# A linear-attention block with a gated feed-forward branch: joint inner products in the last projection, a new chunk layout, and phi's relu on another engine

## The chip, the cores and the metric

The kernel runs on one core of one Trainium2 chip. The metric is the device time of one execution in microseconds (us); for each kernel the median of several executions is given. TensorE is called PE, its weight loads PEld, VectorE DVE, ScalarE ACT, GpSimd POOL, and SyncE, which issues all DMAs here, SP.

## The reference

x is 2048 tokens by 1024 features, in bf16. After a layer norm two branches are computed and joined:

```python
phi = lambda t: where(t > 0, t + 1, exp(t)) + 1e-6
q, k, v = xn @ wqkv            # 32 heads of 32
kv = phi(k).T @ v              # per head
o  = phi(q) @ kv / (phi(q) @ sum(phi(k)) + 1e-6)
s  = o @ wo
g  = silu((silu(xn @ w_gate) * (xn @ w_up)) @ w_down)    # hidden width 3584
out = x + s * g
```

## The kernel before

Nearly every matrix product is made by a seven-product scheme of Strassen's kind. A product of 2 x 2 blocks is made from seven block products of sums and differences of the blocks (R00, R10, R01, R11, T1 to T4 on the token side; A.. and S3, S5, S6, S7 on the weight side) instead of eight. Class `Pair` (line 718) carries it out for a pair of results w = 0, 1: `step(w, m)` makes product m in PSUM, and the results leave through `evac` after products 2, 7, 3 and 4. After products 2, 3 and 4 the evacuation reads PSUM (kind "ps"); product 7's result passes through an SBUF tile first (kind "sb"). Products named in the set J are made for both w at once, by a second level of the same scheme inside: seven *inner* products of 256 columns, whose operands are again sums and differences of quarters. `fresh` (line 748) does this for products 1 and 5 in four steps; `early` (line 857) lists those steps alternately for 5 and 1, and `late` the rest. In `fresh` two ACT copies and two DVE additions of 256 columns lie between the PE steps.

The work goes in stages: layer norm with keys and values (K stage), queries (Q stage), gate and up projections, the attention output s, and last the down projection. Intermediate h and s go to memory and come back.

*phi* is made by `phi_evac` (line 1031): ACT makes exp of the PSUM result into an SBUF tile (line 470), DVE takes min(., 1) + 1e-6 (line 1034), and DVE adds max(src, 0), reading the source again (line 1036). It is used for keys in `kv_out` (line 1047, called with c = 0 or 1 for the two halves of the keys) and for queries in `q_pair` (line 1262): 32 evacuations each.

*The down stage* (lines 1416 to 1584) goes through four couples of token tile pairs, each couple of two pairs w = 0, 1. For each pair it makes the token side's combinations T1 to T4 on DVE (`DProv.comb`, in halves of 896 elements) and then products 1, 5, 6, 2, 7, 3, 4, each 14 matmuls of 128 x 128 weights by 512 columns. Here the tokens are the stationary operand and the down weights move. Each couple needs four chunks of h of 896 KB (`h_load`), in six places `HC`; those of the next couple are loaded after product 5. In the first pair DVE also makes the weight sums S6, S7 and S3 (`wd_comb`). Each of the 32 results is evacuated by `d_pair`: ACT makes silu of the PSUM bank, DVE multiplies by s (loaded by DMA, 128 KB) and adds x (loaded 256 KB at a time), and a DMA stores it.

*What sets the order.* Each operation is first listed with its reads and writes. A planner (class `Plan`) then puts the operations of each engine and of SP in a fixed order by a model of their durations: the one that can start first, by deadline among those that are ready. PE may take operations from a window of 20. A DMA is placed some 12 us ahead of need unless it is marked `asap`. Operations of DVE whose operands are all in SBUF are marked `port`, and the model lets them and POOL's operations exclude each other. On the chip each engine then runs its list in that order, and semaphores hold it where something is not ready. Temporary tiles come from pools of slots: F2 (9 of 2 KB), F1 (4 of 1 KB), H1 (12 of 1 KB) and the 8 PSUM banks; a slot that has been free longest is taken first.

Of the kernel before, what the change touches and what calls it, by code (L numbers as in the profile page):

```python
# [13 lines left out]
KB = 1024  # L14
# [27 lines left out]
class VB:  # L42

    __slots__ = ("pool", "slot", "ops", "left", "armed", "leaves", "r", "id")
    count = 0

    def __init__(self, pool, armed=False, leaves=True):
        self.pool, self.armed, self.leaves = pool, armed, leaves
        self.slot = None
        self.ops = []  # L50
        VB.count += 1
        self.id = VB.count
        self.r = Region([("vb", self.id)])
# [6 lines left out]
class Plan:  # L60
# [62 lines left out]
    def schedule(self):  # L123
# [15 lines left out]
        for o in ops:  # L139
            o.npred = len(o.preds)  # L140
            o.ready = 0.0
            for v in o.vbs:
                if v.ops[0] is o:
                    v.left = len(v.ops)
                    v.pool.pend.append(o.idx)
# [12 lines left out]
        def place(o, t):  # L158
            got = []
            when = o.ready  # L160
            for v in o.vbs:
                if v.slot is not None:
                    continue
                P = v.pool
                mine = [k for u, k in got if u.pool is P]
                if len(P.free) <= bisect_left(P.pend, o.idx) + len(mine):
                    return inf, None
                c = None
                for k in P.free:
                    if v.armed and not P.armed[k] or k in mine:  # L170
                        continue
                    m = max(P.time[k], t)
                    key = (m, P.armed[k] and not v.armed, P.time[k], k)
                    if c is None or key < c[0]:
                        c = (key, k)
                if c is None:
                    return inf, None
                got.append((v, c[1]))
                when = max(when, P.time[c[1]])
            return when, got  # L180
# [118 lines left out]
def build_kernel(nc, A_x, A_wqkv, A_wo, B_w_gate, B_w_up, B_w_down, out, WINDOW=20, NWARM=12, NIDLE=5, LEAD=12.0):  # L299
# [8 lines left out]
    CS, IS = ("dve",) * 4, ("pool",) * 8  # L308
    UBANK, PU = 0.0, 6.0
    N0, NA, WA = 3, 2, True  # L310
    GC0 = ("dve",) * 4
# [10 lines left out]
    with ExitStack() as es:  # L322
# [82 lines left out]
        for k in range(F2.n):  # L405
            for hl in range(4):
                dsem("rr%d_%d" % (k, hl))
        for P in (F2, H1):
            for k in range(P.n):
                dsem("%s_%d" % (P.name, k))  # L410
# [65 lines left out]

        def tt(reads, writes, o, a, b, alu, n, fast=False, eng="dve"):
            f = lambda h: h.tensor_tensor(ev(o), ev(a), ev(b), alu)  # L478
            if eng == "pool":
                return op("pool", reads, writes, f, n / 531.0 + 0.2)  # L480
            q = dve(reads, writes, f, n, 1.92 if fast else 0.96)

            q.port = not any(isinstance(x, VB) and x.pool is BANK for x in reads)
            return q
# [545 lines left out]

        def phi_evac(reads, src, kind, out_ap, out_r):
            e = tmp(H1)
            act(reads, [e], partial(vap, e, FP16), src, ACT.Exp, 512, kind)
            dve([e], [e], lambda h: h.tensor_scalar(vap(e, FP16), vap(e, FP16), 1.0, EPS_PHI, ALU.min, ALU.add),  # L1034
                512, 3.84, urgent=PU).port = True
            dve(reads + [e], [out_r], lambda h: h.scalar_tensor_tensor(  # L1036
                out_ap, ev(src), 0.0, vap(e, FP16), ALU.max, ALU.add), 512, urgent=PU).port = kind == "sb"
# [9 lines left out]
        def kv_out(q, c, reads, src, kind):  # L1047

            if c < 2:
                o = pk_at[q % 4] + c * KB  # L1050
                phi_evac(reads, src, kind, SB.at(o, KB), SB.reg(o, KB))
            else:
# [209 lines left out]
        def q_pair(p, s, wf, at=(), mix=()):  # L1262
            def evac(w, i, j, src, v, kind):
                g = 2 * (2 * s + w) + i
                o, orr = pq_tile(p, g, j)
                phi_evac([v], src, kind, o, orr)
            ST.pair(Pair(Prov(wf, XV[p]), evac, JQ), at, mix)
# [147 lines left out]

        HC = [80, 112, R2, 96, 88, 104]
        HT = [120, 123.5, 127, 74]
        GB = 3584

        def hchunk(c):  # L1420
            o = HC[c] * KB
            return SB.at(o, 2 * GB, FP16).rearrange("p (n t) -> p n t", t=256), o

        def hpart(c, w, lo=0, hi=14):
            v, o = hchunk(c)
            keys = []
            for n in range(lo, hi):
                keys += SB.reg(o + n * 512 + w * 256, 256).keys
            return v[:, lo:hi, w * 128:(w + 1) * 128], Region(keys)

# [4 lines left out]
        def h_load(p, cc, f, c, **kw):  # L1435
            v, o = hchunk(c)
            dma([named("h", p, f)], [SB.reg(o, 2 * GB)], v,
                h_scr[p, f].rearrange("p (n t) -> p n t", t=512)[:, :, cc * 256:(cc + 1) * 256], dsem("hc%d" % c), 896 * KB, **kw)

        class DProv:  # L1440
# [5 lines left out]
            def form(self, nm, lo=0, hi=14):  # L1446
                if nm in ("T2", "T3"):
                    return htile(self.t[nm == "T3"], lo, hi)
                return hpart(self.ch[{"R00": 0, "R10": 1, "T4": 1, "R01": 2, "T1": 2, "R11": 3}[nm]], self.w, lo, hi)

# [5 lines left out]
            def full(self, w, m):  # L1456
                out_ = []
                for lo, hi in ((0, 4), (4, 7), (7, 10), (10, 14)):
                    v, r = self.form(XOF[m], lo, hi)
                    prs, rd = [], [r]  # L1460
                    for n in range(lo, hi):
                        wv, wr = wd_run(WDM[m], n, n + 1, BF16 if WDM[m][0] == "A" else FP16)
                        prs.append((v[:, n - lo, :], wv[:, 0, :]))
                        rd.append(wr)
                    out_.append((prs, rd))
                return out_

        def d_pair(p, m, prov):
            xo = {}

            def evac(w, i, j, src, v, kind):
                t = p * 8 + j * 4 + m
                g, s = tmp(H1), tmp(H1)
                dma([named("s", t, i)], [s], partial(vap, s, FP16), s_scr[t, i], vsem(s), 128 * KB)
                act([v], [g], partial(vap, g, FP16), src, ACT.Silu, 512, kind)
                tt([g, s], [g], partial(vap, g, FP16), partial(vap, g, FP16), partial(vap, s, FP16), ALU.mult, 512, True)
                if j not in xo:
                    q = xo[j] = tmp(F2)
                    dma([], [q], partial(vap, q), xf[t * 128:(t + 1) * 128, :], vsem(q), 256 * KB)
                q = xo[j]  # L1480
                xv = partial(vap, q, BF16, i * KB, KB)
                tt([g, q], [q], xv, partial(vap, g, FP16), xv, ALU.add, 512, True)
                dma([q], [], of[t * 128:(t + 1) * 128, i * 512:(i + 1) * 512], xv, vsem(q), 128 * KB, asap=True)
            return Pair(prov, evac)

# [60 lines left out]

        cur, spare = [0, 2, 1, 3], [4, 5]
        tw = [0]
        pend = []

        def chunks(p, cc, cur, late):
            for f in (0, 2, 1, 3):
                if (f in (1, 3)) == late or late is None:
                    h_load(p, cc, f, cur[f])
        chunks(0, 0, cur, None)
        for q, (p, cc) in enumerate(couples):
            last = None
            for w in range(2):
                t = [(0, 1), (2, 3)][tw[0] % 2]
                tw[0] += 1  # L1560
                pv = DProv(list(cur), w, t)
                pv.comb("T1", "R01", "R00")
                pv.comb("T2", "R11", "T1")
                pv.comb("T3", "T2", "R00")
                P = d_pair(p, 2 * cc + w, pv)
                nxt = couples[q + 1] if q < 3 else None
                for m in (1, 5, 6, 2, 7, 3, 4):
                    P.step(0, m)
                    if m == 2:
                        pv.comb("T4", "R10", "T2")  # L1570
                    if q == 0 and w == 0 and m == 1:
                        wd_comb("S6", "S5", "A00", ALU.subtract, FP16, BF16)
                        wd_comb("S7", "A11", "S6", ALU.subtract, BF16, FP16)
                        wd_comb("S3", "A10", "S6", ALU.subtract, BF16, FP16)
                    if nxt and w == 0 and m == 5:
                        ncur = [spare[0], cur[0], spare[1], cur[2]]
                        h_load(nxt[0], nxt[1], 0, ncur[0])
                        h_load(nxt[0], nxt[1], 2, ncur[2])
                    if nxt and w == 1 and m == 5:
                        h_load(nxt[0], nxt[1], 1, ncur[1])  # L1580
                        h_load(nxt[0], nxt[1], 3, ncur[3])
            if nxt:
                spare = [cur[1], cur[3]]
                cur = ncur

# [67 lines left out]
```

## Time and profile before

| | |
|---|---|
| median of 3 executions | 748.47 us (747.05 to 748.60) |
| the profiled execution | 745.33 us |
| its span, first to last instruction | 743.6 us |
| PE busy | 712.8 us (96%), 4092 matmuls |
| DVE busy | 567.2 us (76%) |
| ACT busy | 357.9 us (48%) |
| POOL busy | 262.0 us (35%) |

The profile is of one execution, with its own time. Busy time is given per engine; matmuls overlap their neighbours, so that a busy PE isn't necessarily at its peak, and the distance from start to start says more than the duration of one (379 ns at 512 columns, 273 at 256). A group's line has line, engine, operation, output<-input, shape and count, then busy us, mean ns of one, and the engine's idle time just before it with what ended it. In a windows view, each row is a stretch of time with its length and each engine's busy us and number of instructions in it. `ps` is a PSUM bank, `SB` the large SBUF array. Some matmul records, a few per cent, are missing from a trace.

### The profile page before, as it was taken

What the parts mean: (1) busy time and instruction counts of PE and PEld (TensorE: products, weight loads), DVE (VectorE), ACT (ScalarE), POOL (GpSimd) and SP (SyncE); (2) the same over time, 40 slices, a digit from 0 to 9 for tenths busy, and PEclk for the clock granted to TensorE, in tenths of its full rate; (3) what the DMA queues carried; (4) which work ended last, traced back from release to release, by engine and by line L of the source; (5) the groups of instructions that cost most, each with busy time, mean ns of one, the idle gap of its engine ahead of it and who ended that gap; (6) DMA issues with size and microseconds to landing.
All of it is one profiled execution on the core that took longest, in us unless ns stands there. A gap on an engine that the chain in (4) does not pass through costs nothing.

```text
span 743.6 us, 11430 instructions
## 1 busy us (share of the span) xinstructions
PE 712.8 (96%) x4092; PEld 385.8 (52%) x4121; DVE 567.2 (76%) x1107; ACT 357.9 (48%) x677; POOL 262.0 (35%) x230
## 2 busy tenths in 40 slices
PE   8999999788999899999999999999999999999996
PEld 4444544344465565566666566566554444444442
DVE  6999766999989899887888888889978562533523
ACT  3567644765646677755545455454664111111111
POOL 2021000137548655876658747520740000000000
PEclk9999999999999999999999999999999999999999
DMA  9844205130233465475331233344698372927421
GB/s 303 206 77 109 44 0 169 52 121 4 67 117 128 153 207 180 133 264 169 104 109 50 93 107 107 93 139 153 214 318 246 114 213 84 277 79 217 125 76 42
DMA packets 139672, 101.54 MB, mean 137 GB/s; under 512 B 18784, under 2 KB 132704, under 8 KB 139616
## 3 DMA queue, kind: packets, MB, share of 16 engines
q1 hardware_dynamic: 139616, 100.82, 45.2%
q8 instruction: 32, 0.52, 0.3%
q14 instruction: 24, 0.20, 0.1%
HBM read 68.16 MB, written 29.49 MB: 131 GB/s over the span
## 4 chain that ended last, share of the span: by engine, by line
PE 75%; DVE 17%; DMA 3%; issue 2%; ACT 2%; SPq 0%; ACTq 0%; DVEq 0%
PE ps L420 75%; DVE SB L478 8%; DVE SB L1036 3%; DVE ps L478 2%; DVE SB L1034 2%; ACT SB L470 1%; DMA SB<-in_A_x_dram 1%; DMA SB<-q_scratch 1%; DMA SB<-SB 1%; DVE stats L995 1%; DVE stats L994 1%; SPq L490 0%; DVE Zh L1205 0%; ACT ps L470 0%; DVE SB L1201 0%
## 5 line engine op out<-in xcount | busy, mean ns | idle before, releaser
L420 PE MATMUL ps<-SB 128*128 128x512 f16 (+3 forms) x3971 | 702.4, 337 | 21.6 <-ACT ps L470 7.7
L420 PEld LDWEIGHTS ps<-SB 128*128 128x128 f16 (+1 forms) x4000 | 379.9, 98 | 342.6 <-DVE SB L478 15.0
L478 POOL TENSOR_TENSOR SB<-SB 128x1024 f16<-128x1024 bf16 (+3 forms) x196 | 247.9, 1292 | 226.5 <-PE ps L420 113.8
L470 ACT ACTIVATE SB<-ps 128x256 f32<-128x256 f32 (+4 forms) x397 | 213.0, 558 | 170.1 <-PE ps L420 157.1
L478 DVE TENSOR_TENSOR SB<-SB 128x512 f16<-128x512 f16 (+10 forms) x312 | 197.7, 662 | 71.7 <-DMA out_dram<-SB 20.6
L478 DVE TENSOR_TENSOR SB<-ps,SB 128x256 f32<-128x256 f32 (+2 forms) x318 | 181.4, 590 | 51.7 <-PE ps L420 41.0
L478 DVE TENSOR_TENSOR ps<-ps,SB 128x512 f32<-128x512 f32 (+1 forms) x238 | 122.2, 529 | 30.7 <-PE ps L420 23.4
L470 ACT ACTIVATE ps<-ps 128x512 f32<-128x512 f32 (+1 forms) x166 | 81.8, 494 | 124.7 <-PE ps L420 95.4
L470 ACT ACTIVATE SB<-SB 128x512 f16<-128x512 f32 (+1 forms) x68 | 42.2, 621 | 79.5 <-DVE SB L478 76.6
L998 POOL TENSOR_TENSOR rstd<-veps,neg_half 128x1 f32<-128x1 f32 x16 | 11.5, 721 | 63.6 <-DVE veps L997 61.0
L1034 DVE TENSOR_SCALAR SB<-SB 128x512 f16<-128x512 f16 x64 | 23.5, 383 | 11.9 <-ACT SB L470 11.9
L1036 DVE SCALAR_TENSOR_TENSOR SB<-ps,SB 128x512 bf16<-128x512 f32 x49 | 32.4, 678 | 0.1
L470 ACT ACTIVATE SB<-SB,zc 128x512 bf16<-128x512 bf16 x32 | 22.2, 715 | 3.2 <-DVE SB L478 3.0
L470 ACT ACTIVATE SB<-SB,nmr,rstd 128x1024 f16<-128x1024 bf16 x12 | 14.7, 1234 | 1.9 <-DVE nmr L1000 1.8
L994 DVE BATCH_NORM_STATS2 stats<-SB 128x6 f32<-128x512 bf16 x16 | 10.9, 683 | 3.4 <-DMA SB<-in_A_x_dram 3.4
L1036 DVE SCALAR_TENSOR_TENSOR SB<-SB 128x512 bf16<-128x512 f32 x15 | 12.5, 842 | 0.0
L995 DVE BATCH_NORM_STATS2 stats<-SB 128x6 f32<-128x512 bf16 x16 | 10.9, 680 | 0.0
L420 PE MATMUL ps<-SB,ident 128*128 128x512 f16 x17 | 6.4, 550 | 1.4 <-POOL ident L501 1.4
L449 PE MATMUL ps<-ident,SB 128*128 128x128 f16 x40 | 3.1, 220 | 1.7 <-DVE SB L1201 1.1
L420 PEld LDWEIGHTS ps<-SB,ident 128*128 128x128 f16 x17 | 2.1, 130 | 4.5 <-issue 2.8
L1286 DVE RECIPROCAL SB<-SB 128x64 f32<-128x64 f32 x8 | 4.3, 539 | 0.0
L449 PEld LDWEIGHTS ps<-ident,SB 128*128 128x128 f16 x40 | 2.4, 98 | 3.6 <-DVE SB L1004 1.6
(28 smaller groups left out, 24.8 us busy)
## 6 DMA issues: line engine op xcount, KB each, us to landing
h_scratch<-SB SPq DMA_DIRECT2D x112, 128.0 KB, 2.3
SB<-h_scratch SPq DMA_DIRECT2D x16, 896.0 KB, 6.5
SB<-in_A_x_dram SPq DMA_DIRECT2D x32, 256.0 KB, 3.2
SB<-in_B_w_gate_dram SPq DMA_DIRECT2D x14, 512.0 KB, 4.1
SB<-in_B_w_up_dram SPq DMA_DIRECT2D x14, 512.0 KB, 5.4
SB<-in_B_w_down_dram SPq DMA_DIRECT2D x4, 1792.0 KB, 8.7
SB<-in_A_wqkv_dram SPq DMA_DIRECT2D x12, 512.0 KB, 8.4
SB<-r_scratch SPq DMA_DIRECT2D x32, 128.0 KB, 2.8
```

What stands on the lines that cost most here:

```text
L420: last = h.matmul(o() if callable(o) else o, l() if callable(l) else l, r() if callable(r) else r, start=st, stop=sp, skip_group_check=True)
L449: last = h.transpose(o(), i(), ident[:, :])
L470: return op("act", reads, writes, lambda h: h.activation(ev(o), ev(i), func, **kw), n / 1200.0 + (0.055 if src == "ps" else 0.095) + (0.09 ...
L478: f = lambda h: h.tensor_tensor(ev(o), ev(a), ev(b), alu)
L994: dve([xr] + ([named("ve", 0)] if q == 1 else []), [sA], lambda h: h.bn_stats(stats[:, j, 0, :], xa[:, 0:512]), 512)
L995: dve([xr] + ([named("ve", 0)] if q == 1 else []), [sB], lambda h: h.bn_stats(stats[:, j, 1, :], xa[:, 512:1024]), 512)
L998: pool([ver, nh_r], [rsr], lambda h: h.tensor_tensor(rstd[:, j, :], veps[:, j, :], neg_half[:, :], ALU.pow), 0.56)
L1034: dve([e], [e], lambda h: h.tensor_scalar(vap(e, FP16), vap(e, FP16), 1.0, EPS_PHI, ALU.min, ALU.add), 512, 3.84, urgent=PU).port = True
L1036: dve(reads + [e], [out_r], lambda h: h.scalar_tensor_tensor(out_ap, ev(src), 0.0, vap(e, FP16), ALU.max, ALU.add), 512, urgent=PU).port = ...
L1286: dve([ea], [ra], lambda h, q=q: h.reciprocal(vap(ra, F32)[:, q * 64:q * 64 + 64], vap(ea, F32)[:, q * 64:q * 64 + 64]), 400)
```

## The change

Two things change. First, phi's relu: where `relu` is set, ACT makes it from the same source into a second tile, and DVE adds the two SBUF tiles. That is the case for the first half of the keys (c = 0) and for those query evacuations that read PSUM.

```diff
+    RQ = lambda w, i, j, kind: kind == "ps"
+    RK = lambda q, c, kind: c == 0
...
-        def phi_evac(reads, src, kind, out_ap, out_r):
+        def phi_evac(reads, src, kind, out_ap, out_r, relu=False):
             e = tmp(H1)
             act(reads, [e], partial(vap, e, FP16), src, ACT.Exp, 512, kind)
             dve([e], [e], lambda h: h.tensor_scalar(vap(e, FP16), vap(e, FP16), 1.0, EPS_PHI, ALU.min, ALU.add),
                 512, 3.84, urgent=PU).port = True
+            if relu:
+                r = tmp(H1)
+                act(reads, [r], partial(vap, r, FP16), src, ACT.Relu, 512, kind)
+                tt([e, r], [out_r], out_ap, partial(vap, e, FP16), partial(vap, r, FP16), ALU.add, 512, True)
+                return
             dve(reads + [e], [out_r], lambda h: h.scalar_tensor_tensor(
                 out_ap, ev(src), 0.0, vap(e, FP16), ALU.max, ALU.add), 512, urgent=PU).port = kind == "sb"
```

Second, the down stage. The first couple is made as before. In the other three, both pairs of a couple are one `Pair` with J = (1, 5): products 1 and 5 are made jointly by inner products. `DJProv.inner` makes the token side's inner sums for a couple (four additions of 896 elements for each of the two products), `wd_inner` the weight side's, once (eight of 1792 elements, one of each four in place). T1 to T4 are made for both pairs at once, with halves of 1792. After the joint steps come products 2, 6, 7, 3, 4, each for w = 0 and then w = 1.

Memory is laid out anew. There are five chunk places instead of six; a next couple's chunk goes into the only spare place (f = 0) or into one that this couple has finished with (f = 2 after T1, f = 3 after product 7, f = 1 after product 3), and is marked `asap`. T2 has a place of its own, T3 takes that of R00. The inner sums lie in gaps, and, from the second couple on, in two slots of F2 and four of H1 (`gone`), which are taken for good when the first such sum is made: a tile with `only=k` can have slot k alone, and a sum that holds several of them starts when all are free. An evacuation loads its 128 KB of x itself, into a slot of F1.

```diff
-        HC = [80, 112, R2, 96, 88, 104]
-        HT = [120, 123.5, 127, 74]
+        HC = [80, 112, 199, 96, 87]
+        HT = [119, 122.5, 103, 106.5]
+        H2 = 103
+        HI_AT = [73.5, 75.25, 77, 94, 110, 129.5, 194, 195.75]
+        WI_AT = [70, 160, 163.5, 126, 119, 122.5]
+        gone = [VB(F2, only=k) for k in range(2)] + [VB(H1, only=k) for k in range(8, 12)]
...
+        def wd_inner(m):
+            raw = BF16 if WDM[m][0] == "A" else FP16
+            R = {(h, u): wq(m, h, u, raw) for h in range(2) for u in range(2)}
+            d = wq(m, 0, 1, FP16)
+            t2, t3, t4 = (wi(m, f) for f in range(3))
+            for o, a, b in ((t3, R[1, 1], R[0, 1]), (d, R[0, 1], R[0, 0]), (t2, R[1, 1], d), (t4, R[1, 0], t2)):
+                tt([a[1], b[1]], [o[1]], o[0], a[0], b[0], ALU.subtract, 1792, True, hold=gone[:2] if m == 1 else ())
...
+            def inner(self, m):
+                B = {(k, w): self.form(XOF[m], 7 * k, 7 * k + 7, w) for k in range(2) for w in range(2)}
+                n0, n1, n2, s5 = (self.hi(m, f) for f in range(4))
+                for o, a, b, alu in ((n1, B[0, 0], B[0, 1], ALU.subtract), (s5, B[0, 1], B[1, 1], ALU.add),
+                                     (n0, s5, B[0, 0], ALU.subtract), (n2, B[1, 0], n0, ALU.subtract)):
+                    tt([a[1], b[1]], [o[1]], o[0], a[0], b[0], alu, 896, True, hold=gone[2:] if m == 5 else ())
...
-                g, s = tmp(H1), tmp(H1)
+                g, s, x = tmp(H1), tmp(H1), tmp(F1)
...
+            ncur = [spare, cur[3], cur[2], cur[0]]
+            if q == 0:
...
+                        if w == 0 and m == 5:
+                            load(1, 0, ncur[0])
+                        if w == 1 and m == 5:
+                            load(1, 2, ncur[2])
+                            load(1, 3, ncur[3])
+                            wd_inner(1)
+                            wd_inner(5)
+                        if w == 1 and m == 3:
+                            load(1, 1, ncur[1])
+            else:
+                pv = DJProv(list(cur))
+                P = d_pair(p * 8 + 2 * cc, pv, (1, 5))
+                pv.inner(1)
+                pv.comb("T1", "R01", "R00")
+                pv.inner(5)
+                load(q + 1, 0, ncur[0])
+                for _, st in P.early():
+                    st()
+                pv.comb("T2", "R11", "T1")
+                pv.comb("T3", "T2", "R00")
+                load(q + 1, 2, ncur[2])
+                for m in (2, 6, 7, 3, 4):
+                    for w in range(2):
+                        P.step(w, m)
+                    if m == 2:
+                        pv.comb("T4", "R10", "T2")
+                    if m == 7:
+                        load(q + 1, 3, ncur[3])
+                    if m == 3:
+                        load(q + 1, 1, ncur[1])
+            spare, cur = cur[1], ncur
```

## The prediction

> **What bounds the kernel now.** I read the down stage first, since most of the diff lies there. The chain that ended last, from 540 us on, starts with its shares by line (first fence, first line). Then it names only matmuls until the last three steps, which are the last evacuation. The windows view (second fence) has 92 to 94 matmuls of 512 columns in every 20 us and DVE mostly idle.
>
> ```profile
> by line: PE ps L420 96.5%; issue 0.4%; DVE SB L478 0.4%; ACT SB L470 0.3%
> ...
> 705.71 10.74 PE ps L420 x49
> 716.45 0.05 issue
> 716.50 10.74 PE ps L420 x49
> ```
>
> ```profile
> core 0: us, PE busy (x) PEld busy (x) DVE busy (x) ACT busy (x) POOL busy (x), PEclk, DMA share, GB/s
> 20.00:60.00 40.00, 37.50 (x193) 16.73 (x196) 38.24 (x92) 25.19 (x40) 5.02 (x6) 1.00 0.60 137
> 140.00:200.00 60.00, 52.19 (x339) 26.44 (x339) 58.41 (x117) 38.13 (x76) 30.64 (x23) 1.00 0.23 70
> ...
> 600.00:620.00 20.00, 19.89 (x92) 9.06 (x93) 9.47 (x20) 3.60 (x6) 0.00 (x0) 1.00 0.56 164
> ```
>
> So the down stage is bound by the number of PE columns alone. Start to start, neighbouring 512-column matmuls in the trace stand 215 or 216 ns apart; 784 of them (8 tile pairs x 7 products x 14) are 169.0 us, and counted back from PE's end at 737.6 the stage began at 568.7 and couple 1 begins at 568.7 + 2 x 21.1 = 610.9.
>
> Where phi is evacuated it is otherwise: in the K stage (20 to 60 us) and the Q stage (140 to 200 us) DVE is busy 96% and 97% and PE idles 2.5 and 7.8 us. The timeline of the Q stage shows two costs that the relu edit trades, and a collision:
>
> ```profile
> 169.78 4.62 POOL L478 TENSOR_TENSOR SB<-SB 128x512 f16<-128x512 f16 x4
> ...
> 170.54 4.02 DVE L1034 TENSOR_SCALAR SB<-SB 128x512 f16<-128x512 f16 x4
> ...
> 191.14 2.47 DVE L1036 SCALAR_TENSOR_TENSOR SB<-ps,SB 128x512 bf16<-128x512 f32 x4
> 193.54 1.08 DVE L478 TENSOR_TENSOR SB<-SB 128x512 f16<-128x512 f16 x3
> ```
>
> Four of the old last steps of phi take 2.47 us, a single one 0.68, so one follows the next after (2.47 - 0.68)/3 = 0.60. Of plain SBUF additions three take 1.08, one 0.42: 0.33 each. But at 170.5 four tensor_scalars of SBUF data, each 0.20 when undisturbed, take 4.02 us beside four POOL additions, and PE waits 2.2 us behind them. The groups by form give the average of it: the tensor_scalar from 120 to 200 us, and, over the whole kernel, a two-input operation of SBUF data against the same with one input in PSUM (number after the bar: busy us, mean ns).
>
> ```profile
> L1034 DVE TENSOR_SCALAR SB<-SB 128x512 f16<-128x512 f16 x32 | 14.5, 487 | 1.7 <-ACT SB L470 1.7
> ```
>
> ```profile
> L478 DVE TENSOR_TENSOR SB<-ps,SB 128x512 f16<-128x512 f32 x84 | 57.3, 683 | 9.2 <-ACT SB L470 8.6 <-PE ps L420 0.2
> ...
> L478 DVE TENSOR_TENSOR SB<-SB 128x512 f16<-128x512 f32 x28 | 30.7, 1097 | 0.0
> ```
>
> The form with an input in PSUM is not stretched; the one of SBUF alone is.
>
> [...] ten 256-column matmuls take 1.25 us at 345.28, one 0.272, so (1.25 - 0.272)/9 = 0.109. [...]
>
> **The change part by part.**
>
> *Joint products, PE.* A couple's products 1 and 5 were 2 x 2 x 14 = 56 matmuls of 512: 56 x 0.2155 = 12.07 us. They become 2 x 7 x 7 = 98 of 256: 98 x 0.109 = 10.68. Every one loads its weights; 98 ns of load fit under 109, and runs of twelve keep that pitch. Gain 1.39 us, three couples: **-4.2 us**, all of it on the path, since nothing else ends there. The first couple stays as it was.
>
> *Chain within the joint steps.* Elsewhere these steps are woven with the pair before; here 98 stand nearly alone, products 5 and 1 alternating. A step of two inner products takes PE 1.53 us; in that time ACT's 256-column copies (0.37 and 0.38) or DVE's addition (0.42) must come back[...]. Some 0.7 us is spare; a 1.1 us combination just ahead on DVE costs at most 0.4. Two or three such hits: +0.3 at most +1; I take **0**, as the model orders DVE around them, and keep +1.
>
> *Combinations on DVE.* Interpolating the 896-wide (620 ns) and 2048-wide (1213) rows, a 1792-wide one is 1.08 us. New once: 8 of these for the weights, 8.6 us. New per couple: 8 of 896, 5.0 us; T1 to T4 halve in number and double in width: equal. In couples 2 and 3 DVE has over 20 of 41 us free and the chunks land a whole phase ahead: 0. In the switch from couple 0 to 1 it is tight. The third chunk (f=2) now goes into the place of T1, free once the second tile's product 5 is done: 589.8 + 6.0 = 595.8. Landing takes 6.1 us in the median (8.3 at most), behind another 896 KB that may be ahead on SP's queue (up to 3.8 at the 241 GB/s of 590 to 612): 602 to 606. T1 (2.2) and the first two additions of inner(5) (1.2) follow, with some 2 us of evacuations between: 607 to 611.5, due 610.9. **+0.5 us**, from 0 to 2. Its cover is the weights being done by then: 16 us of new DVE work, of which 4 to 7 can go before 590, in 20 us with 6 to 8 us of other work. Behind a chunk load that waits on SP's queue stand s and x loads and output stores; PE waits for none of them.
>
> *Slots.* From here F2 loses two slots and H1 four. PE waits for none directly: silu frees the bank, and it needs one of 8 H1 slots where about 5 are in use. x comes in 32 loads of 128 KB instead of 16 of 256: SP issues 16 more of 0.43 us, 7 us in 170; behind them stand the s and h loads and the stores. F1 has 4 slots; load 3.2, add and wait about 1.5, store 1.9 with its queue about 2: under 9 us a round, so 4 slots give an evacuation every 2.2 us; the closest need is one in 3.0. 0.
>
> *phi's relu, K stage.* 16 evacuations. DVE gives up 0.60 and takes 0.33: -0.27 each. ACT gains one 512-column read of PSUM, 0.50 to 0.595: 8 us in a stage where it is 63% busy. About half fall before 55 us, where the chain runs through DVE: -2.0 at best; afterwards PE is full and nothing counts. POOL is nearly idle, so no collision. PE waits for ACT too there: I take **-0.8** (0 to -2.0).
>
> *phi's relu, Q stage.* 24 evacuations (products 2, 3, 4 of 32 in all). Undisturbed: 24 x -0.27 = -6.4 us of DVE. But the old step reads PSUM and keeps 0.60 beside POOL; the new addition is SBUF alone, and POOL is busy 51%. The tensor_scalars there average 487 ns, 0.2 us over the 0.28 of an undisturbed one. With 0.2 on each addition: 24 x (0.53 - 0.60) = -1.6 us. ACT rises from 38.1 to 50 of 60 us; behind the relus queue the copies and drains that PE waits for, 5 to 6 us in all of these 60. For it: the bank is free after two ACT reads instead of after three steps on two engines. I take **-1.2**; from below -5 (no collision), from above +9.6 (each addition meets a POOL operation as the four at 170.5 did: 1.0 us, 24 x 0.4).
>
> Sum: -4.2 + 0 + 0.5 - 0.8 - 1.2 = -5.7 us. The profiled execution took 745.33 (span 743.6, 1.7 around it) and would take 739.6. It lies 3.1 under the median of the runs, 748.47, which becomes **742.8**. About 0.2%, 1.5 us, is what a measurement can tell from none.
>
> **Rivals.**
> - *Relu brings nothing* (K and Q cancel against ACT's queue): -3.7, 744.8. For it: 51% POOL; against: the earlier bank.
> - *Relu brings its full worth*: Q -5, K -1.5, so -10.2, 738.3. For it: DVE at 97%; against: the collision seen at 170.5.
> - *The switch stalls.* inner(5) may start only when H1's slots 8 to 11 are free together; slots are handed out oldest first, and about four of twelve are in use by s loads made up to 12 us ahead. If the four are scattered it waits for a lull, up to some 5 us; PE can run product 1's steps meanwhile but without the alternation. +4.5: -1.2, 747.3, no change.
> - *Slower[...].* Q's additions at 1.0 on an engine that is 97% busy: +9.6 - 0.8 - 3.7 = +5.1, 753.6. It ends level at an addition of 0.60 + 4.5/24 = 0.79 us and is slower beyond 0.85. Against it: order is made by a plan that counts an SBUF addition and POOL as excluding each other, and DVE has other work to put in between.
>
> **How the numbers follow.** Forecast 0.52 (own range 740.5 to 744.5), nothing from relu 0.19, full worth 0.08, stalled switch 0.12, slower 0.09. Faster 0.79, within 0.2% 0.12, slower 0.09. Forecast and first rival hold 0.71; to 739.0 and 747.2, half of the two next on either side come in, 0.81.
>
> **What would show it.** Right: the down stage's PE in 164.8 us: 616 matmuls of 512 columns and 294 of 256; no PE gap above 1 us near 611; DVE's line 1036 with about 24 instructions instead of 64 in all; PE's idle time in 140 to 200 us down by 1 to 2. Wrong: new SBUF additions of phi averaging over 0.8 us; ACT over 90% in the Q stage; PE waiting for an addition of inner(5) or a chunk at the switch; 256-column pitch above 115 ns when they stand alone.

## The result, and the profile after

| | before | changed |
|---|---|---|
| median of 4 executions | 747.87 us | 748.22 us (746.96 to 749.63) |
| ratio, 95% interval | | 1.0005 (0.9981 to 1.003) |
| profiled execution, span | 745.33, 743.6 us | 749.63, 747.9 us |

No change that can be measured, where 5.7 us less was forecast (742.8 from 748.47). The profiled execution of the changed kernel is the slowest of its four and that of the kernel before a fast one, so stages are compared by their own lengths and the verdicts rest on medians and ratios.

The windows view of the changed kernel, for the stretches shown of before:

```profile
core 0: us, PE busy (x) PEld busy (x) DVE busy (x) ACT busy (x) POOL busy (x), PEclk, DMA share, GB/s
20.00:60.00 40.00, 40.00 (x221) 19.24 (x220) 38.65 (x99) 29.60 (x48) 5.57 (x8) 1.00 0.58 139
140.00:200.00 60.00, 50.81 (x307) 27.07 (x308) 53.15 (x115) 46.19 (x97) 30.99 (x24) 0.97 0.23 68
600.00:620.00 20.00, 20.00 (x119) 11.36 (x117) 15.18 (x25) 3.54 (x7) 0.00 (x0) 1.00 0.57 166
```

In the K stage PE no longer idles between 20 and 60 us. In the Q stage DVE fell from 58.4 to 53.2 us of 60 and ACT rose from 38.1 to 46.2, as the edit would have it. But PE is busy 50.8 us where it was 52.2, and its clock is no longer full (0.97). The groups from 120 to 200 us say what became of phi on DVE:

```profile
L1038 DVE TENSOR_SCALAR SB<-SB 128x512 f16<-128x512 f16 x32 | 15.4, 503 | 2.8 <-ACT SB L474 2.8
L482 DVE TENSOR_TENSOR SB<-SB 128x512 bf16<-128x512 f16 x23 | 8.7, 416 | 0.0
```

These 23 of the 24 new additions take 416 ns each, as undisturbed ones do (418 in e8 below, where POOL is busy 17.2 us from 125 to 200 us, 31.1 in e5). The last one falls just outside: it starts at 200.08 us beside POOL's additions, takes 2.33 us, and PE waits for it:

```profile
197.74 6.70 POOL L482 TENSOR_TENSOR SB<-SB 128x1024 f16<-128x1024 f16 x5
...
199.70 2.71 DVE L482 TENSOR_TENSOR SB<-SB 128x512 bf16<-128x512 f16 x2
...
202.47 1.06 PE L424 MATMUL ps<-SB,Zh 128*32 128x256 bf16 x32 [1.63 <-DVE SB L482]
```

PE's longest gap in this stage has another origin:

```profile
170.27 5.34 DVE L1038 TENSOR_SCALAR SB<-SB 128x512 f16<-128x512 f16 x7
170.43 9.05 POOL L482 TENSOR_TENSOR SB<-SB 128x512 f16<-128x512 f16 x8 [0.86 <-DVE SB L482]
...
175.54 1.63 DVE L1045 SCALAR_TENSOR_TENSOR SB<-SB 128x512 bf16<-128x512 f32 x1
177.09 0.69 DVE L482 TENSOR_TENSOR ps<-ps,SB 128x512 f32<-128x512 f32 x1
...
177.84 2.53 PE L424 MATMUL ps<-SB 128*128 128x512 f16 x7 [3.19 <-DVE ps L482]
```

Seven tensor_scalars in a row, four before, run beside POOL's additions and take 0.28 to 1.26 us each, 1.24 in the median (0.28 undisturbed, in e8), one more operation of SBUF data follows with 1.63 us (0.68 undisturbed), and behind them stands the PSUM addition that PE awaits: a gap of 3.19 us (2.16 before). The first 512-column matmuls after it stand 0.43 us apart, twice the 0.215 of before; the granted clock is 0.50 from 177.2 to 180.6 us.

Of the down stage, the chain that ended last, from 600 to 640 us:

```profile
by line: PE ps L424 83.5%; DMA out_dram<-SB 14.7%; SPq L494 1.3%; ACT SB L474 1.0%; issue 0.3%
...
615.84 0.52 SPq L494
616.37 0.04 issue
616.41 5.88 DMA out_dram<-SB
622.28 0.02 issue
622.31 0.39 ACT SB L474
622.70 0.05 issue
622.75 17.39 PE ps L424 x104
```

An output store releases an ACT operation, and that releases PE. The timeline has both waits:

```profile
622.31 0.87 ACT L474 ACTIVATE SB<-ps 128x256 f32<-128x256 f32 x2 [5.86 <-DMA out_dram<-SB]
...
622.75 5.52 PE L424 MATMUL ps<-SB 128*128 128x256 bf16 x49 [1.62 <-ACT SB L474]
```

I count the stage from the fourth matmul of its product 1 to PE's end: that is 168.7 us in every profiled execution with the old down stage, and 167.7 in the changed kernel, 1.0 us less. (The expectation of e11 below counts from the issue of the last s store, which gives 167.1 here; that issue depends on SP's queue.)

### The profile page after: what moved, and what is told of

It is laid out like the page before. It is cut to its first block, busy times and chain, and to the rows that moved or that the text cites. A ratio compares the mean times of both kernels' runs of the same rounds, so it can differ in the third digit from the quotient of the medians.

```text
span 747.9 us, 11806 instructions
## 1 busy us (share of the span) xinstructions
PE 712.4 (95%) x4247; PEld 399.7 (53%) x4247; DVE 587.8 (79%) x1127; ACT 380.2 (51%) x729; POOL 261.9 (35%) x230
## 4 chain that ended last, share of the span: by engine, by line
PE 70%; DVE 14%; DMA 7%; ACT 5%; issue 3%; SPq 0%; DVEq 0%; ACTq 0%
PE ps L424 70%; DVE SB L482 9%; ACT SB L474 4%; DMA SB<-h_scratch 2%; DVE ps L482 2%; DMA out_dram<-SB 1%; DVE SB L1038 1%; DMA SB<-SB 1%; DMA SB<-in_A_x_dram 1%; DMA SB<-q_scratch 1%; ACT ps L474 1%; DVE SB L1045 1%; DMA m_scratch<-SB 1%; SPq L494 0%; DVE SB L1210 0%
## 5 line engine op out<-in xcount | busy, mean ns | idle before, releaser
L424 PE MATMUL ps<-SB 128*128 128x512 f16 (+4 forms) x4126 | 702.1, 331 | 24.2 <-DVE ps L482 8.3
L424 PEld LDWEIGHTS ps<-SB 128*128 128x128 f16 (+1 forms) x4126 | 393.9, 98 | 330.2 <-DVE ps L482 17.5
L474 ACT ACTIVATE SB<-ps 128x256 f32<-128x256 f32 (+5 forms) x443 | 235.0, 566 | 143.9 <-PE ps L424 113.9
L482 DVE TENSOR_TENSOR SB<-SB 128x512 f16<-128x512 f16 (+11 forms) x360 | 237.1, 691 | 56.7 <-ACT SB L474 23.0
L482 DVE TENSOR_TENSOR ps<-ps,SB 128x512 f32<-128x512 f32 (+1 forms) x250 | 127.8, 525 | 26.1 <-PE ps L424 16.9
L474 ACT ACTIVATE ps<-ps 128x512 f32<-128x512 f32 (+1 forms) x172 | 84.4, 492 | 122.5 <-PE ps L424 91.3
L474 ACT ACTIVATE SB<-SB,zc 128x512 bf16<-128x512 bf16 x32 | 22.3, 717 | 6.2 <-DVE SB L482 6.1
L1045 DVE SCALAR_TENSOR_TENSOR SB<-ps,SB 128x512 bf16<-128x512 f32 x9 | 6.0, 681 | 0.0
```

The costliest lines, as they stand in the source:

```text
L424: last = h.matmul(o() if callable(o) else o, l() if callable(l) else l, r() if callable(r) else r, start=st, stop=sp, skip_group_check=True)
L474: return op("act", reads, writes, lambda h: h.activation(ev(o), ev(i), func, **kw), n / 1200.0 + (0.055 if src == "ps" else 0.095) + (0.09 ...
L1045: dve(reads + [e], [out_r], lambda h: h.scalar_tensor_tensor(out_ap, ev(src), 0.0, vap(e, FP16), ALU.max, ALU.add), 512, urgent=PU).port = ...
```

## The experiments

All ran in several rounds; the ratio is to the kernel before on the same chip, with its 95% interval.

| run | median, us | before, us | ratio (interval) |
|---|---|---|---|
| e1 relu, keys and queries | 749.86 | 747.76 | 1.0027 (1.0015, 1.0038) |
| e2 down stage alone | 746.31 | 747.76 | 0.9982 (0.9969, 0.9995) |
| e3 relu, keys | 746.73 | 747.76 | 0.9977 (0.996, 0.9993) |
| e4 down stage, x in F2 | 744.57 | 747.76 | 0.9954 (0.9938, 0.997) |
| e5 relu, queries | 750.89 | 748.40 | 1.0031 (1.0015, 1.0047) |
| e6 the same by way of PSUM | 753.37 | 748.40 | 1.0056 (1.0028, 1.0083) |
| e7 before, short POOL | 743.00 | 748.40 | 0.9913 (0.9879, 0.9948) |
| e8 relu, queries, short POOL | 740.18 | 748.40 | 0.9886 (0.9848, 0.9924) |
| e9 e4 and relu, keys | 743.82 | 747.71 | 0.9936 (0.9911, 0.996) |
| e10 e5 without head start | 748.56 | 747.71 | 1.0005 (0.9984, 1.0025) |
| e11 whole change, x in F2 | 745.48 | 747.71 | 0.9963 (0.9947, 0.9979) |
| e12 e11 without head start | 744.36 | 747.71 | 0.9946 (0.9927, 0.9965) |
| e13 unused relu | 753.90 | 748.45 | 1.0065 (1.0042, 1.0088) |
| e14 unused relu, short POOL | 745.61 | 748.45 | 0.996 (0.9942, 0.9979) |
| e15 before without head start | 752.85 | 748.45 | 1.0057 (1.0037, 1.0077) |

### Taking the change apart: e1 to e4

e1 is the kernel before with `phi_evac` of the changed one; e3 has it with `RQ` never true, e2 is the changed kernel with both never true:

```diff
-    RQ = lambda w, i, j, kind: kind == "ps"
-    RK = lambda q, c, kind: c == 0
+    RQ = lambda w, i, j, kind: False
+    RK = lambda q, c, kind: False
```

e4 is e2 with the x tile elsewhere:

```diff
-                g, s, x = tmp(H1), tmp(H1), tmp(F1)
+                g, s, x = tmp(H1), tmp(H1), tmp(F2)
```

In the expectations, port operations are DVE's operations that the plan marks `port`, and their collisions are what befell the four at 170.5 us in the kernel before: 0.55 to 1.24 us each beside POOL's additions, against 0.28 in e8.

Expected of e1: 

> The kernel before with the relu edit alone (keys c = 0, queries after products 2, 3, 4). Theory A (the new SBUF additions of the Q stage stand behind POOL's[...]): slower than before by 2 to 5 us, with several port operations in a row beside POOL and a PE gap above 2 us between 150 and 200 us. Theory B (the loss lies in the down stage alone, relu works as forecast): faster by about 2 us. Theory C (neither; the plan's order only shifted): within 1 us of before.

Expected of e2: 

> The changed kernel with the old phi everywhere, so the down stage's edit alone. Theory A (relu lost what the down stage gained): faster than before by 2 to 3 us, that is 4.2 us of columns less some 2 us in which PE waits for an F1 slot. Theory B (the down stage lost its own gain): within 1 us of before. Before about 600 us its trace should run as that of the kernel before, within 0.5 us.

Expected of e3: 

> The kernel before with the relu edit on the first half of the keys alone. POOL is nearly idle in that stage, so theory A expects no loss: between 0 and 2 us faster, 0.8 by the forecast. If the relu edit harms by ACT's longer queue[...], this one is slower too, by 1 us or more.

Expected of e4: 

> The down stage's edit alone, with the x tile of an evacuation in a slot of F2 and not of F1. Theory: the joint steps' ACT copy waits for an F1 slot that an output store still holds, because x tiles now share the four F1 slots with it. Then the PE gap of 1.6 us at the start of couple 1 and the one of 0.5 us at couple 2 go, and the kernel is 1.5 to 2.5 us faster than the down edit alone, 3.5 to 4.5 faster than before. Rival: the gaps come from ACT or DVE being late anyway; then no difference above 0.5 us.

Relu as a whole costs 2.1 us, the down stage gains 1.5, the keys gain 1.0, and with x in F2 the down stage gains 3.2, a little less than the 3.5 to 4.5 expected. The parts add up to the whole: -1.5 + 2.1 = 0.6 against 0.35. Each of the theories held for its own part: relu lost time, and the down stage lost half of its own gain (1.5 left of 3.2). One expectation failed: e2's down stage begins 1.6 us later in its trace than that of the kernel before, not within 0.5, so only the length of the stage is compared. e2's timeline has the slot wait without any relu before it (the idle time and its releaser stand in brackets):

```profile
618.03 0.87 ACT L474 ACTIVATE SB<-ps 128x256 f32<-128x256 f32 x2 [3.72 <-DMA out_dram<-SB]
...
618.47 1.70 PE L424 MATMUL ps<-SB 128*128 128x256 f16 x14 [0.88 <-ACT SB L474]
```

The ACT operation of 256 columns is the copy of an inner product into the tile `s` of `fresh`, and that tile comes from F1. In e4 the down stage takes 165.1 us instead of 166.9, and no gap of PE in it exceeds 0.2 us. The difference of 1.8 us agrees with that of the medians, 1.7. Only `x` was moved, so the rival, that ACT or DVE is late anyway, falls.

### Does the slot explain the changed kernel too, and do the good parts add up: e11, e9

e11 is the changed kernel with x in F2, e9 is e4 with relu for the keys. Both, and e12, also correct a line of the planner, so that a slot that must be a certain one is taken off the waiting list whichever of its users comes first. In e11 the plan comes out the same with the old line, so that the place of x alone separates it from the changed kernel.

```diff
-                v.pool.pend.remove(o.idx)
+                v.pool.pend.remove(v.ops[0].idx)
```

Expected of e11: 

> The changed kernel whole, relu for keys and queries, with x tiles in F2. The slot theory: its down stage, 167.1 us in the changed kernel, takes about 164.5 as in the down edit with F2 alone, and PE's gap of 1.6 us at the start of couple 1 is gone; so 2 to 3 us faster than the changed kernel (748.2), near 745.7. Rival: another wait takes the place of the slot's, within 1 us of 748.2.

Expected of e9: 

> The down stage's edit with x tiles in F2, and the relu edit on the keys alone: the parts that gained by themselves. If they add up (3.2 and 1.0 by the medians of the two runs): 4 us faster than before, near 743.5. If they share one gain: no faster than the down edit with F2 alone, 744.6.

e11 is at 745.48, 2.7 us under the changed kernel's 748.22 (0.42% by the ratios, whose intervals don't meet); its down stage takes 164.9 us instead of 167.7. The chain from 600 us on has no store and hardly anything but matmuls:

```profile
by line: PE ps L424 96.6%; DVE SB L482 0.6%; ACT SB L474 0.4%; issue 0.4%
```

e9 adds up as well: 743.82, 3.9 us under before (3.2 + 1.0 expected). It is faster than the kernel before by 0.64%, where the changed kernel is level with it.

### The queries: e5, e6

e5 has relu for the queries alone. In e6 ACT writes relu back and DVE reads PSUM as it used to:

```diff
-                r = tmp(H1)
-                act(reads, [r], partial(vap, r, FP16), src, ACT.Relu, 512, kind)
-                tt([e, r], [out_r], out_ap, partial(vap, e, FP16), partial(vap, r, FP16), ALU.add, 512, True)
+                act(reads, reads, src, src, ACT.Relu, 512, kind)
+                tt(reads + [e], [out_r], out_ap, src, partial(vap, e, FP16), ALU.add, 512)
```

Expected of e5: 

> The kernel before with the relu edit on the queries alone. By the runs of both and of the keys alone (749.9 and 746.7 us against 747.8) it is to be slower than before by about 3 us, with PE's gap of some 3 us near 174 us in its trace. If the two parts act on each other instead, it is within 1 us of before.

Expected of e6: 

> As the run of the queries alone, but ACT writes relu back into the PSUM bank and DVE's addition reads the bank: the same extra ACT work, the old 0.6 us on DVE[...]. Theory A[...]: most of the loss goes, within 1.5 us of before. Theory D (ACT's longer queue, which PE waits behind, costs the time): as slow as the queries alone or slower, 3 us or more over before, since DVE has no gain to set against it.

e5 is 2.5 us slower, and its trace has the same 3.19 us gap, at 175.1 us. e6 is 5.0 us slower, so theory A in its simple form falls: without a new operation of SBUF data alone the loss did not go. e6 says little more, since with relu in place the bank is also held until DVE's addition has read it (0.68 us each), and its clock was the lowest of all (0.988 in the profiled execution).

### POOL and ACT apart: e7, e8, e13, e14

For the first two gate and up weights POOL's sums are made one column wide, on a tile that nothing else uses (`tiny`); reads, writes and waits stay. These kernels leave those sums out.

```diff
+            if eng == "pool" and short[0]:
+                return op("pool", reads + [nh_r], writes + [named("tiny")], lambda h: h.tensor_tensor(
+                    tiny[:, :], neg_half[:, :], neg_half[:, :], ALU.mult), 0.2)
```

In e13 and e14 ACT makes the 24 relus and nobody reads them; DVE does its old steps.

```diff
                 act(reads, [r], partial(vap, r, FP16), src, ACT.Relu, 512, kind)
-                tt([e, r], [out_r], out_ap, partial(vap, e, FP16), partial(vap, r, FP16), ALU.add, 512, True)
-                return
```

Expected of e7: 

> The kernel before, with POOL's operations for the first two gate and up weights (inner sums of both, combinations of the second) made one column wide on a tile of their own, so that these sums are left out[...]. Theory A (port collisions already cost the Q stage time before the change): faster than before by 2 to 5 us. If the collisions are hidden, within 1 us.

Expected of e8: 

> The relu edit on the queries alone, with the same POOL operations made one column wide (those sums are left out). Theory A: without POOL the edit gains what the plain sum says, so that it is faster than the kernel before with short POOL operations by 1 to 5 us, where with POOL it was slower by 3. Theory D (ACT): slower than that one by 2 us or more, as with POOL.

Expected of e13: 

> The kernel before, with the 24 relus of the queries made by ACT but read by nobody: ACT's new work alone, DVE as before[...]. Theory A (order of DVE's operations beside POOL): within 1 us of before. Theory D (ACT's longer queue): slower by 2 us or more.

Expected of e14: 

> The same unused relus, with POOL's operations for the first two gate and up weights one column wide (those sums are left out), to be set against the kernel before with short POOL operations (743.0 us). Theory A: within 1 us of that. Theory D: slower by 2 us or more, as with POOL at work.

e7 gained 5.4 us, a little over the 2 to 5 expected, e8 is 2.8 under e7, e13 lost 5.5 and e14 is 2.6 over e7. By their ratios the six kernels make a table of two steps, in per cent of before:

| | POOL as it is | POOL short |
|---|---|---|
| old phi | 0 | -0.87 |
| and ACT's relu, unused | +0.65 | -0.40 |
| relu used, DVE relieved | +0.31 | -1.14 |

Downwards, ACT's new work costs 0.65% (4.9 us), and 0.47% (3.5 us) with short POOL; DVE's relief then gives back 0.34% (2.5 us) or 0.74% (5.5 us). Theory D, for which I had little, has both of its runs on its side: beside POOL, ACT's work costs more than DVE's relief is worth. With short POOL the relief is worth more; but the difference, 0.27%, is not clear of noise (the intervals of e7 and e8 overlap), so it isn't shown that POOL decides the sign. The plan also orders each of the six kernels anew, and every step contains that; see e15 below.

DVE's groups from about 140 to 204 us show POOL's part, first in e5, then in e8, and last the tensor_scalar of the kernel before:

```profile
L1036 DVE TENSOR_SCALAR SB<-SB 128x512 f16<-128x512 f16 x27 | 14.0, 544 | 1.2 <-ACT SB L472 1.1
L480 DVE TENSOR_TENSOR SB<-SB 128x512 bf16<-128x512 f16 x24 | 10.9, 494 | 0.0
```

```profile
L482 DVE TENSOR_TENSOR SB<-SB 128x512 bf16<-128x512 f16 x24 | 9.3, 418 | 1.6 <-ACT SB L474 1.6
...
L1041 DVE TENSOR_SCALAR SB<-SB 128x512 f16<-128x512 f16 x27 | 7.5, 283 | 1.3 <-ACT SB L474 1.2
```

```profile
L1034 DVE TENSOR_SCALAR SB<-SB 128x512 f16<-128x512 f16 x27 | 13.2, 523 | 0.0
```

The additions are stretched by 76 ns on average beside POOL; as in the changed kernel that is a single one of 2.3 us, the others take 0.41 to 0.42. The tensor_scalars are stretched by 261, but so they are in the kernel before: that is no cost of the edit.

ACT's part can be seen in the chain that ended last, from 130 to 215 us, of the kernel before and of the changed one:

```profile
by line: PE ps L420 36.2%; DVE SB L1036 17.6%; DVE SB L478 13.6%; DVE SB L1034 12.2%; DVE ps L478 8.5%; DVE Zh L1205 3.1%; ACT SB L470 2.5%; DVE SB L1286 2.2%; DVE SB L1201 1.5%; issue 1.3%; ACT ps L470 1.2%; DVE SB L1284 0.4%; ACTq L294 0.
```

```profile
by line: PE ps L424 44.4%; ACT SB L474 17.6%; DVE SB L1038 9.4%; DVE SB L482 7.0%; DMA m_scratch<-SB 4.6%; DVE ps L482 4.2%; DVE SB L1045 3.8%; ACT ps L474 3.2%; issue 2.6%; ACT L474 1.5%; DVE SB L1210 0.9%; PE ps L453 0.7%; ACTq L296 0.0%
```

ACT rises from 3.7 to 22.3% of it. The new entry, a DMA, points to a suspect that no run tests alone. Relu's second tile takes a slot of H1, and the tiles that the m_scratch and r_scratch stores send out lie in H1 too. In the kernel before, ACT waits for no DMA from 120 to 215 us; in the changed kernel it waits 3.2 us for such stores (3.1 in e5), and PE once behind it:

```profile
139.49 1.57 ACT L474 ACTIVATE SB<-ps 128x512 f16<-128x512 f32 x3 [1.28 <-DMA m_scratch<-SB]
...
140.14 0.61 PE L424 MATMUL ps<-SB 128*128 128x512 bf16 x3 [1.22 <-ACT SB L474]
```

It isn't the whole loss, since e6 has no second tile, no such wait, and lost time as well. In e13, where the loss is larger, ACT has only 6.0% of that chain, and one of its gaps is mixed:

```profile
154.65 4.26 POOL L480 TENSOR_TENSOR SB<-SB 128x1024 f16<-128x1024 bf16 x2 [1.77 <-PE ps L422]
...
156.49 3.53 ACT L472 ACTIVATE SB<-ps 128x512 f16<-128x512 f32 x7
156.62 2.63 DVE L1036 TENSOR_SCALAR SB<-SB 128x512 f16<-128x512 f16 x3 [0.60 <-ACT SB L472]
...
160.74 1.32 PE L422 MATMUL ps<-SB 128*128 128x512 bf16 x5 [1.63 <-DVE SB L1041]
```

DVE waits 0.60 us for ACT, which then has seven reads of PSUM in a row; but of DVE's three tensor_scalars one takes 2.2 us beside POOL, and PE awaits a step behind them. So what the unused relu costs isn't ACT's time alone either.

### Order alone: e10, e12, e15

The plan gives phi's tensor_scalar a head start of 6 us (`PU`). It was taken from the queries with relu in e10 and e12, and from the kernel before in e15:

```diff
-                512, 3.84, urgent=PU).port = True
+                512, 3.84, urgent=0.0 if relu else PU).port = True
```

Expected of e10: 

> The relu edit on the queries alone, with the plan's head start of 6 us for phi's tensor_scalar taken from those queries, so that it and the new addition queue alike. Theory A2 (what costs the time is a run of such SBUF operations beside POOL, placed ahead of an addition that PE awaits): the 3.2 us gap near 174 us goes or halves and the kernel is 1 to 4 us faster than with the head start (750.9). Rival (the collisions cost the same wherever they stand, or ACT does): within 1 us of it.

Expected of e12: 

> The changed kernel whole with x tiles in F2 and without the head start for the queries' tensor_scalar. If theory A2 holds: 1 to 4 us faster than the same with the head start, and perhaps the fastest of all. If not: equal to it.

Expected of e15: 

> A control: the kernel before, with the plan's head start of 6 us for phi's tensor_scalar taken from the queries and nothing else. If a mere change of order in the Q stage moves the time as much as the relu edit did (2.5 us), the time that the edit lost cannot be put down to its operations; if within 1 us of before, it can.

e10 is 0.26% under e5 by ratio (1.9 us), at the lower end of what was expected and with intervals that overlap, and its gap at 172 us is 2.4 us instead of 3.2. But a larger one arose at 195.4, from six of the new additions in a row beside POOL:

```profile
192.30 7.86 DVE L480 TENSOR_TENSOR SB<-SB 128x512 bf16<-128x512 f16 x6
193.16 8.99 POOL L480 TENSOR_TENSOR SB<-SB 128x1024 f16<-128x1024 bf16 x4 [13.49 <-DMA SB<-in_B_w_up_dram]
...
200.21 1.90 PE L422 MATMUL ps<-SB,Zh 128*32 128x256 bf16 x32 [4.79 <-DVE SB L480]
```

So moving such a run only moved the collision: three of the six additions take 2.33 us each, the others 0.42. e12 is 0.17% under e11, with intervals that overlap: nothing to tell. The control e15 is the sobering one: with no operation added or removed, the order alone costs 0.57% (4.4 us). That is the size of the table's steps (0.34 to 0.74%; the intervals of two of the four don't meet, those of the other two just do) and more than the 2.5 us of the relu edit. By what was laid down for e15 beforehand, the loss of e5 cannot be put down to its operations.

e10 and e15 can also be set against each other. Both lack the head start (e10 for the 24 tensor_scalars with relu, e15 for all 32), and only e10 has relu: 1.0005 (0.9984 to 1.0025) against 1.0057 (1.0037 to 1.0077). In that order relu for the queries gains some 0.5%, where with the head start it loses 0.31%. So even the sign of its worth depends on the order that the plan chose around it. How the 2.5 us divide between ACT's work, POOL, the H1 slots and the order stays open.

## Why the prediction was wrong

Its sum had seven terms. Five of them held, one of these somewhat short.

- *Joint products, -4.2 us of columns.* Nearly right: where x lies in F2, 168.7 us became 164.9 to 165.3 (e4, e9, e11, e12), 3.4 to 3.9 us less. The pitch of 256 columns is 0.109 us in e11's joint steps too.
- *Chain within the joint steps, 0.* Right, but for the slot: in e11 PE has no gap above 0.12 us in that stage. The 0.7 us of spare time in a step was my estimate.
- *Switch to couple 1, +0.5 us.* 0 to 0.2; and the rival of the stalled switch, with H1's slots, didn't come. It named 747.3, close to the result, by a mechanism that no run shows: that would have been luck.
- *phi's relu, keys, -0.8.* Right: -1.0 by the medians of e3, -1.7 by its ratio.
- *Combinations on DVE, hidden.* Right; DVE was busy 88.4 of the 150 us from 580 to 730 in the changed kernel, and PE waited for it 0.1 us.
- *Slots, "PE waits for none directly", 0.* Wrong: **+1.8 us in the down edit alone, +2.8 in the changed kernel** (166.9 in e2 against 165.1 in e4, 167.7 against 164.9 in e11). I had counted the rate at which x tiles pass through F1, not who else takes from it. `fresh` writes a tile of F1 in its first step, and PE waits for that copy: it must be made before PE goes on in the bank. With x tiles there, the slot comes free only when an output store has landed (5.9 us of DMA in the chain above). The profile of before couldn't show it, for x lay in F2; the code did, in the list of `tmp(F1)`.
- *phi's relu, queries, -1.2 us.* Wrong: **+2.5** (e5). The term was DVE's busy time, 24 x (0.53 - 0.60), and the failing step is that it was taken for the length of a stage in which three engines work on a chain with few banks. DVE's busy time did fall, by 4.1 us from 130 to 215 us in e5 (81.8 to 77.7), and the stretching of each addition, 0.2 us in the sum, was 0.08 on average. But "ACT rises from 38.1 to 50 of 60 us" was left at nothing because ACT stayed below full (it rose to 46.2), and so were the slot that relu's tile takes and the new order. The unused relu alone costs 3.5 to 4.9 us (e14, e13), a change of order alone 4.4 (e15); which of them makes the 2.5 is not shown. ACT's table loads stayed as they were, two of 1283 ns in either kernel.

None of the four signs of being wrong came: the new additions averaged 0.42 to 0.5 us and not over 0.8, ACT was at 77% in the Q stage and not over 90, nothing waited for inner(5) or a chunk, the pitch held. They were averages, or looked at the wrong wait. Of the signs of being right two failed: PE had a gap of 1.62 us in the joint steps of couple 1, and its idle time from 140 to 200 us rose from 7.8 to 9.2 us.

The sum of what was measured, -3.9 + 2.8 - 1.0 + 2.5 = 0.4 us, is the result (0.35). Relu's two terms are known to about 1.2 us each, by the intervals of e3 and e5.

## What to carry to other kernels

When a tile moves to another pool, list everyone who takes from that pool, and ask for the one that PE waits for; a DMA that frees its slot can then stand in PE's chain, as the store of 5.9 us did here. In a stage where two engines share the steps between matmuls, don't price an operation moved from the one to the other by the busy time of the first: ask what it delays on the receiving engine, whatever that engine's share of busy time, and which slot its new tile takes. And where a planner sets the order, a control that only reorders tells how much of a difference of a few us can be put down to the operations at all.

## What the runs showed of the hardware

A gap of PE can come with a lower clock and so cost more than its length. In the changed kernel the clock was 0.72 from 175 to 180 us and 0.94 in the next 5, at the end of the 3.19 us gap: it was 0.50 for 3.4 us, from 177.2 to 180.6, and that is up to 1.7 us of full clock. In e1's profiled execution PE was idle for 3.5 us of the stretch from 170 to 180 us (3.2 in the changed kernel), and the clock stayed at 1.00. From 260 to 265 us the changed kernel's clock was 0.75 too (0.50 from 259.1 to 262.5), after a gap of only 1.95 us, and the kernel before has a gap of 2.12 there with the clock at 1.00. So the length of a gap alone doesn't tell whether the clock falls.

The granted clock differs from one execution to the next: over 162 executions of the kernel before it lies between 0.989 and 1.000, and the time is longer by about 0.6 us for each 0.001 that it is lower. The mean clock was 0.996 there, 0.995 in e5, 0.994 in e15, 0.993 in e13 and 0.992 in e6. By that slope an estimated 1.0, 1.1, 1.7 and 2.7 us of these four runs' losses come by way of the clock.

Phi's new additions were stretched by a lot or not at all: beside POOL's additions of 1024 columns (2.2 us each) one takes either its 0.42 us or 2.33, with nothing between in e5 and e10.
